# Pairs of 64-row matmuls, LN transposes by DMA and a DMA-shifted V in a fused attention and gated-MLP kernel

## The chip, the cores and the metric

The kernel runs on one core of one Trainium2 chip. The metric is device time in microseconds (us) of one launch; lower is better. Each version ran four or five times, interleaved with the kernel before (three to seven times) on the same chip, and medians are quoted with the lowest and highest time. "Span" is the length of the profiled execution from its first to its last instruction; the time of a launch is about 1.7 us longer.

## The reference

There are two blocks: a layer norm (LN), windowed attention and a residual; then a second LN, a gated MLP that mixes tokens with a 2048x2048 matrix, and a residual. All data is bf16.

```python
# x [2048, 448]; 16 heads of 28; window 8, dilation 2
qkv  = LN(x) @ wqkv                               # 448 -> 3*448
o    = softmax(q . k[pos - 2*(0..7)] * scale) @ v # eight keys per query, masked before 0
h    = x + o @ wo                                 # 448 -> 448
z    = gelu(LN(h) @ w_in)                         # 448 -> 1792
z1, z2 = z[:, :896], LN(z[:, 896:])
g    = w_sp @ z2 + b_sp[:, None]                  # 2048 x 2048 over the tokens
out  = h + (z1 * g) @ w_out                       # 896 -> 448
```

## The kernel before

The program is written as a graph of steps. Each step has one or more candidate engines with a modelled duration, the buffers it reads and writes, and a priority. A list scheduler in Python places the steps one after the other: it takes the engine that can start first, and on it the step of lowest priority number. The result is a fixed order of instructions for each engine, with semaphore waits between engines. All DMAs are issued by one queue (SyncE, SP), in order.

The parts that the change touches, with cuts:

```python
DC, NCH, NQ, PAD, NAB = 112, 4, 114, 14, 18    # K = 448 as four chunks of 112 rows
xhT = sb("xhT", [DC, NCH, TOKBUF], BF16)       # LN output, transposed, tokens contiguous

def layernorm(m, i, prio):                     # a block of 128 tokens
    ...                                        # statistics and normalise on VectorE -> tring
    # four transposes on PE, then one evacuation into xhT by ScalarE or VectorE

def qk_tile(tc, g8, prio):                     # z1 and z2 have the same form
    G.add([("pe", pe_us(4, 512))], [
        lambda e, c=c: e.matmul(bank(b, 512), wsrc[:, c, gg, :], xhT[0:DC, c, col0:col0 + 512],
                                start=(c == 0), stop=(c == NCH - 1)) for c in range(NCH)], ...)

def att_block(i):                              # 114 queries, 128 keys: 18 overlapping windows
    G.add([("pe", pe_us(4, D))], [             # V straight at the window's own tokens
        lambda e, c=c: e.matmul(bank(b, D, 0, nk), xhT[0:DC, c, t0:t0 + nk], stg[:, c, 2*D:3*D], ...)
        for c in range(NCH)], ...)
    ...                                        # logits, exp, mask, E @ V, transpose
```

Everything up to the last output projection (q/k, V, logits, exp, mask, E @ V, output projection, second LN) is called the attention stage here. After it come z2 with its LN, z1, and then the g and output matmuls.

The softmax here doesn't subtract the row's maximum and nothing guards it: scores larger than these inputs give would overflow.

## Time and profile before

| | before |
|---|---|
| time, median of 3 runs | 265.75 us (265.65 to 268.64) |
| PE / VectorE / ScalarE busy | 97 / 58 / 40% of the span |
| attention stage ends (last output projection) | 97.3 us |
| g and output matmuls end | 259.8 us |

From the page of the kernel before: the span, the busy times of the engines, the busy tenths of PE in 40 slices, the clock granted to PE in tenths, and what the chain of work that ended last consists of.

```profile
span 263.0 us, 4647 instructions
PE 255.1 (97%) x1868; PEld 129.8 (49%) x1868; DVE 152.4 (58%) x342; ACT 106.3 (40%) x204; POOL 46.6 (18%) x123
PE   6899999999998999999999999999999999999995
PEclk9999999999999999999999999999999999999999
PE 89%; DMA 3%; DVE 3%; ACT 2%; SPq 1%; POOL 1%; issue 0%; DVEq 0%
```

PE (the tensor engine) is the limit from beginning to end, at full clock. The windows view of the same kernel gives, for a stretch of time, its length and each engine's busy time in it, then the granted clock, the DMA share and GB/s:

```profile
60.00:80.00 20.00, 20.00 (x269) 12.24 (x267) 18.05 (x39) 17.20 (x36) 4.08 (x8) 1.00 0.01 2
97.20:117.50 20.30, 20.30 (x117) 10.87 (x117) 20.25 (x54) 14.17 (x26) 10.07 (x26) 1.00 0.25 46
```

In the middle of the attention stage PE is busy for all 20 us, VectorE (third pair of columns) for 18.05 and ScalarE for 17.20. A faster PE would soon meet them. Between 60 and 80 us the DMA queue does nothing (share 0.01). Three pieces of the chain of waits, in order of time (start, duration, what):

```profile
52.81 0.77 PE psum L535 x4
53.58 1.73 PE psum L524 x8
55.31 0.76 PE psum L596 x4
```

They are one V group, two q/k groups and one output projection. Each group pays for four matmuls, though K = 448 fills only 3.5.

### The profile page before, as it was taken

The numbers are of one execution on the slowest core, as the hardware profiler recorded it, in microseconds if no ns is written. First come the engines' busy times: TensorE is split into PE (matmuls) and PEld (weight loads), VectorE is DVE, ScalarE is ACT, GpSimd is POOL, SyncE is SP. The second block draws the span as 40 slices with busy tenths as digits, with TensorE's granted clock in tenths as the row PEclk, the third lists the DMA queues.
The fourth block names the chain that finished last, engine by engine and source line by source line (L and its number), as shares of the span: only waits on it lengthen the run. The fifth ranks groups of instructions, "written<-read, shape, count | busy, mean of one in ns | idle before, by whom it ended". The sixth has DMA issues, their size and how long they took to land.

```text
span 263.0 us, 4647 instructions
## 1 busy us (share of the span) xinstructions
PE 255.1 (97%) x1868; PEld 129.8 (49%) x1868; DVE 152.4 (58%) x342; ACT 106.3 (40%) x204; POOL 46.6 (18%) x123
## 2 busy tenths in 40 slices
PE   6899999999998999999999999999999999999995
PEld 2445665556655555554444444444544444444442
DVE  4697999979979999999431333131513133222233
ACT  1468979779979976772011000111010100010100
POOL 8676013221211125555000000000000000000000
PEclk9999999999999999999999999999999999999999
DMA  6999945000001213213000344401445200200002
GB/s 172 325 261 241 137 99 66 2 0 2 2 0 24 62 43 44 54 42 49 12 0 0 70 98 98 125 4 38 101 100 84 70 0 0 72 0 0 0 2 70
DMA packets 42182, 16.91 MB, mean 64 GB/s; under 512 B 35248, under 2 KB 41584, under 8 KB 42160
## 3 DMA queue, kind: packets, MB, share of 16 engines
q1 hardware_dynamic: 42160, 16.61, 29.3%
q8 instruction: 15, 0.25, 0.4%
q14 instruction: 7, 0.06, 0.1%
HBM read 6.37 MB, written 1.84 MB: 31 GB/s over the span
## 4 chain that ended last, share of the span: by engine, by line
PE 89%; DMA 3%; DVE 3%; ACT 2%; SPq 1%; POOL 1%; issue 0%; DVEq 0%
PE psum L667 37%; PE psum L524 10%; PE psum L632 9%; PE psum L654 9%; PE psum L685 8%; PE psum L596 4%; PE psum L535 4%; DMA x_tm<-in_A_x_dram 3%; PE psum L496 2%; PE psum L569 2%; PE psum L547 2%; ACT E L556 2%; PE psum L582 1%; DVE st L486 1%; DVE tring L491 1%; SPq L440 0%
## 5 line engine op out<-in xcount | busy, mean ns | idle before, releaser
L672 DVE TENSOR_TENSOR ub<-psum,bb 128x512 bf16<-128x512 f32 x28 | 19.4, 691 | 82.7 <-PE psum L667 82.7
L659 ACT ACTIVATE z1p<-psum 128x512 bf16<-128x512 f32 x28 | 16.7, 597 | 114.1 <-PE psum L654 114.1
L667 PE MATMUL psum<-wsp,z2p 128*128 128x512 bf16 x224 | 51.0, 379 | 0.0
L667 PE MATMUL psum<-early,z2p 128*128 128x512 bf16 x224 | 50.8, 379 | 0.0
L556 ACT ACTIVATE E<-psum 128x456 bf16<-128x456 f32 (+1 forms) x72 | 35.0, 562 | 1.4 <-PE psum L547 1.2
L667 PEld LDWEIGHTS psum<-wsp,z2p 128*128 128x128 bf16 x224 | 21.8, 98 | 26.5
L667 PEld LDWEIGHTS psum<-early,z2p 128*128 128x128 bf16 x224 | 21.9, 98 | 26.4
L524 PE MATMUL psum<-xhT,early 112*128 112x512 bf16 x128 | 30.5, 379 | 0.1
L654 PE MATMUL psum<-xhT,w_in 112*128 112x512 bf16 x112 | 28.8, 378 | 0.0
L514 POOL TENSOR_TENSOR rstd<-va,mhalf 128x1 f32<-128x1 f32 x48 | 27.7, 580 | 3.2
L512 POOL TENSOR_SCALAR va<-mv 128x1 f32<-128x1 f32 x48 | 13.2, 283 | 72.8 <-DVE mv L488 62.0
L632 PE MATMUL psum<-w_in,xhT 112*128 112x448 bf16 x128 | 25.5, 352 | 0.0
L685 PE MATMUL psum<-w_out,z1p 128*128 128x448 bf16 x112 | 21.8, 352 | 0.0
L486 DVE BATCH_NORM_STATS2 st<-x_tm 128x6 f32<-128x448 bf16 x32 | 19.2, 610 | 2.6 <-DMA x_tm<-in_A_x_dram 2.5
L637 ACT ACTIVATE z2p<-psum 128x448 bf16<-128x448 f32 x32 | 17.1, 544 | 7.2 <-PE psum L632 7.2
L564 DVE TENSOR_TENSOR E<-E,maskb 128x1824 bf16<-128x1824 bf16 (+1 forms) x18 | 19.6, 1089 | 0.0
L640 DVE BATCH_NORM_STATS2 st<-z2p 128x6 f32<-128x448 bf16 x32 | 18.1, 596 | 0.0
L654 PEld LDWEIGHTS psum<-xhT,w_in 112*128 112x128 bf16 x112 | 10.9, 97 | 13.3
L524 PEld LDWEIGHTS psum<-xhT,early 112*128 112x128 bf16 x128 | 11.5, 97 | 12.0 <-ACT V L508 0.2
L632 PEld LDWEIGHTS psum<-w_in,xhT 112*128 112x128 bf16 x128 | 12.1, 98 | 10.3
L535 PE MATMUL psum<-early,xhT 112*128 112x448 bf16 (+1 forms) x72 | 16.1, 352 | 0.8 <-DVE xhT L509 0.8
L685 PEld LDWEIGHTS psum<-w_out,z1p 128*128 128x128 bf16 x112 | 11.0, 98 | 10.4
(59 smaller groups left out, 245.7 us busy)
## 6 DMA issues: line engine op xcount, KB each, us to landing
out_dram<-tring SPq DMA_DIRECT2D x16, 112.0 KB, 1.8
w_in<-in_B_w_in_dram SPq DMA_DIRECT2D x1, 1568.0 KB, 13.8
x_tm<-in_A_x_dram SPq DMA_DIRECT2D x1, 896.0 KB, 10.0
early<-in_A_wqkv_dram SPq DMA_DIRECT2D x1, 784.0 KB, 6.0
w_out<-in_B_w_out_dram SPq DMA_DIRECT2D x1, 784.0 KB, 15.5
bb<-in_B_b_sp_dram SPq DMA_DIRECT2D x1, 512.0 KB, 13.2
wsp<-in_B_w_sp_dram SPq DMA_TRANSPOSE x32, 2.8
early<-in_B_w_sp_dram SPq DMA_TRANSPOSE x32, 2.7
```

The source lines that it names most:

```text
L486: G.add([("dve", dve_us(D))], [lambda e: e.bn_stats(st[:, s.slot, 0:6], x_tm[:, m, :])], [r_x[m]], [s], [s], prio=prio)
L514: G.add([("pool", 0.61)], [lambda e: e.tensor_tensor(rstd[:, k:k + 1], va[:, k:k + 1], mhalf[:, 0:1], ALU.pow)], [r_va[k], r_half], [r_rs[ ...
L524: lambda e, c=c: e.matmul(bank(b, 512), wsrc[:, c, gg, :], xhT[0:DC, c, col0:col0 + 512], start=(c == 0), stop=(c == NCH - 1)) for c in ra ...
L535: lambda e, c=c: e.matmul(bank(b, D, 0, nk), xhT[0:DC, c, t0:t0 + nk], stg[:, c, 2 * D:3 * D], start=(c == 0), stop=(c == NCH - 1)) for c ...
L556: lambda e, hh=hh: e.activation(E[0:nk, ev.slot, hh * 4:(hh + 1) * 4, 0:nq], bank(lb[hh], 512, 0, nk).rearrange("p (g c) -> p g c", c=128) ...
L564: lambda e: e.tensor_tensor(E[0:nk, ev.slot, :, 0:nq], E[0:nk, ev.slot, :, 0:nq], maskb[0:nk, mi:mi + 1, 0:nq].to_broadcast([nk, NHEAD, nq ...
L632: lambda e, c=c, b=b, h=h, m=m: e.matmul(bank(b, D), xhT[0:DC, c, PAD + 128 * m: PAD + 128 * m + 128], w_in[:, c, FH + D * h: FH + D * (h ...
L640: lambda e, h=h, m=m, s=s: e.bn_stats(st[:, s.slot, 6 * h:6 * h + 6], z2p[:, m, D * h:D * (h + 1)])],
L654: lambda e, c=c: e.matmul(bank(b, 512), w_in[:, c, fc * 128:(fc + 1) * 128], xhT[0:DC, c, PAD + 512 * tc: PAD + 512 * (tc + 1)], start=(c ...
L667: lambda e, s=s: e.matmul(bank(b, 512), z2p[:, s, fc * 128:(fc + 1) * 128], w[:, s, :], start=(s == 0), stop=(s == NB - 1)) for s in range ...
L672: G.add([("dve", dve_us(512))], [lambda e: e.tensor_tensor(ub[:, u.slot, :], bank(b, 512), bb[:, 512 * tc:512 * (tc + 1)], ALU.add)], [b, ...
L685: lambda e, f=f: e.matmul(bank(b, D), z1p[:, f, 128 * m:128 * m + 128], w_out[:, f, :], start=(f == 0), stop=(f == FC7 - 1)) for f in rang ...
```

## The change

The intent is to take work off PE. K = 448 becomes seven chunks of 64 rows. Two products are computed at once, one on the upper and one on the lower 64 rows of the array, in seven steps instead of two times four. The lower half needs the same data on the other 64 partitions, so there is a half-swapped copy xS of the transposed LN output xB. Most LN transposes move from PE to DMA. V is computed once per 128 tokens, in 16 groups rather than 18, and DMAs shift it into the 18 windows. The diff, cut to its core (weight layouts and loads, semaphore reuse and tile aliasing are left out):

```diff
-        xhT = sb("xhT", [DC, NCH, TOKBUF], BF16)
+        xB = sb("xB", [128, NB, NCH, 128], BF16)       # per block; chunks of 128,128,128,64 rows
+        xS = sb("xS", [128, NB, NCH, 128], BF16)       # the two 64-row halves swapped
         def layernorm(m, i, prio):
+            if i or m >= NPT:                          # NPT = 8: 24 of the 32 blocks
+                dma_t(lambda: xB[:, m, :, :], lambda: tring[:, t.slot, :], 1.26, ...)   # DMA transpose
+                if m % 2: ...                          # two DMAs swap the halves of a pair of blocks
+                return
             ...                                        # blocks 0 to 7: on PE as before,
+            ...                                        # and two half copies by VectorE or ScalarE
+        def pair(b, ws, xs, n):
+            return [lambda e, j=j, u=u: e.matmul(bank(b[j], n), ws(j, (LO, HI)[j], u), xs(j, (LO, HI)[j], u),
+                        start=(u == 0), stop=(u == 6), tile_position=(64 * j, 0)) for u in range(7) for j in range(2)]
+        def full(b, ws, xs, n):                        # V and the output projection
+            return [lambda e, c=c, ps=ps: e.matmul(bank(b, n), ws(ps, c), xs(ps, c), ...)
+                    for c, ps in ((0, ALL), (1, ALL), (2, ALL), (3, LO))]    # the last on 64 rows
+        def v_tile(m, prio): ...                       # V of 128 tokens -> ring Vt of 4 slots
         def att_block(i):
-            ...                                        # V at the window's own tokens
+                dma(lambda e, ...: e.dma_start(V1[p0:p0 + n, v.slot, :, :], Vt[q0:q0 + n, ...]),
+                    e1 - k0, [vbuf[m]], ...)           # 34 shifts, one or two per window
+        # model: a DMA costs max(0.45, kb/300) us of the queue and lands 1.7 us later;
+        # a change of tile mode on PE costs 0.1 us; warm-up matmuls are fillers of lowest priority
+        # all z1 pairs are placed before the g matmuls
```

## The prediction

> **What bounds the kernel now.** TensorE (PE). The page's busy line gives PE 255.1 of 263.0 us (97%), VectorE 58%, ScalarE 40%; the chain of waits is 89% PE. By windows, the attention stage (15 to 100 us) loads all three: PE 99%, VectorE about 78 of 85 us, ScalarE about 71. After it only PE is loaded.
>
> In the PE timeline a 512-column matmul costs 216 ns start to start, a 448-column one 189 ns, whether 112 or 128 rows are used. K=448 as 4x112 pays for 4 passes but fills 3.5.
>
> **What the change does to PE.**
> - q/k, z2, z1: a pair of tiles takes 7 steps of two 64-row matmuls in place of 8 full ones. If the halves overlap fully this saves 1/8: 27.6 to 24.2, 24.2 to 21.2, 24.2 to 21.2 us: -9.4 us. The Trainium skill ("TensorEngine Tiling (Array Packing)", Key Properties) says that tiles execute independently. This trace agrees for 32-row tiles: in the logits' matmuls groups of four tiles of 114 columns start about 50 ns apart, the time of one.
> - V: 18 overlapping blocks become 16, -1.5 us.
> - LN transposes: 24 of 32 blocks leave PE (0.22 to 0.27 us each): -6 us; their evacuations (0.60 us on ScalarE or 0.42 on VectorE) go too, about 12 us of the two engines.
> - Cost: the same section says that changing the tiling mode drains the array. Around the logits' matmuls about 0.1 us is lost each way; with an estimated 30 to 40 more switches: +3 to +4 us.
>
> Sum of PE work: about 244 before, 227 after, plus switches.
>
> **Elsewhere.** The start: x blocks 2 and 3 arrive late now (VectorE waits 2.1 us) and q/k begins at 14.8 us. Four blocks now come before the weights, and warm-up becomes filler: -1 to -2 us. Against it: 16 half copies (estimate 0.2 to 0.6 us each), and a DMA queue that gains 24 transposes (1.3 us each, from the batch of 16 in 21.1 us), about 35 V shifts and 24 swaps (0.4 to 0.5 us each): near 90 us of issue before attention ends, full but in time, as w_sp loads can slip behind z2/z1. Landing (1.8 to 2.8 us) lengthens each LN chain; other pairs cover it.
>
> **How much is critical.** Nearly all PE time. z2/z1: -6 us in full. The attention stage would lose about 11 us of PE work, but switches and VectorE/ScalarE (which lose only about 8 us net together) give back 3 to 5: about -7. Start: -1.5. Total about -15 us: 250.5 us, range 245 to 257. Faster by over 2%: 0.93; within 2%: 0.06; slower: 0.01.
>
> **What would show it.**
> - Groups by shape show 64-row matmuls, 224 each for q/k and z2, 196 for z1; a pair takes 1.5 us (512 columns) or 1.33 (448).
> - First q/k at 12 to 13.5 us; last output projection ends near 89 us (97.2 before); z1, now in one run, ends near 129; the g and output matmuls behind it keep about 118 us.
> - PE busy near 240 us; waits for VectorE, ScalarE or the V shift a few us; for w_sp none.
>
> **What would make it wrong.** The 64-row halves may not overlap fully (weight loads not hidden, or PSUM writes): at 1.7 us a pair the gain shrinks to about 7 us. The in-order DMA queue may block: a V shift or LN transpose behind w_sp transposes would stall PE. SBUF transposes may be slower than 1.3 us. Better than told: VectorE and ScalarE keep up, and the stage gets its whole 11 us.

## The result and the profile after

The time is **283.81 us** (median of 4 runs, 281.90 to 285.73) beside 265.7 us of the kernel before in the same rounds (264.77 to 268.64). The ratio is 1.0661, with a 95% interval from 1.0549 to 1.0773: slower. Ratios here are the mean time of one kernel's fast runs over that of the other's of the same rounds, so they are not quite the ratio of the medians that stand beside them. Executions over 1.5% slower than the fastest of the same kernel are left out of the means. The prediction was wrong in its direction.

The same lines of the page, after:

```profile
span 282.7 us, 5079 instructions
PE 258.9 (92%) x2036; PEld 119.9 (42%) x2036; DVE 155.9 (55%) x351; ACT 95.6 (34%) x187; POOL 51.6 (18%) x119
PE   6499977997699879997999999999999999999995
PEclk9689997999579978998899999999999999999999
PE 80%; DMA 6%; POOL 4%; DVE 3%; SPq 2%; ACT 2%; issue 1%; DVEq 0%; ACTq 0%; POOLq 0%
```

PE now has holes in the first half, and its clock drops there too. PE's busy time did not fall, because matmuls at half clock count double. The windows of the kernel after (columns as before) say where:

```profile
15.00:40.00 25.00, 24.92 (x256) 11.33 (x255) 22.03 (x62) 17.86 (x35) 10.18 (x24) 0.97 0.82 142
60.00:80.00 20.00, 15.79 (x156) 6.44 (x154) 11.40 (x25) 8.73 (x18) 3.04 (x6) 0.78 0.58 135
100.00:121.00 21.00, 19.55 (x229) 9.32 (x223) 17.82 (x39) 13.09 (x26) 6.05 (x10) 0.84 0.57 107
121.00:137.50 16.50, 13.90 (x127) 6.95 (x123) 16.39 (x45) 8.45 (x19) 9.32 (x24) 0.90 0.60 119
137.50:161.50 24.00, 23.96 (x225) 12.73 (x226) 9.58 (x24) 16.59 (x32) 5.34 (x13) 1.00 0.22 49
161.50:279.30 117.80, 117.80 (x561) 54.57 (x560) 39.35 (x70) 1.09 (x2) 0.00 (x0) 1.00 0.22 54
```

Between 60 and 80 us PE, VectorE and ScalarE are all busy for less time than before (15.79, 11.40 and 8.73 us against 20.00, 18.05 and 17.20). None of the three is full, so the stage waits for something else. The DMA share went from 0.01 to 0.58. From 137.5 us on nothing is wrong: 224 paired matmuls run without a gap in 24.0 us, and g with the output takes 117.8 us, where the prediction said about 118.

The last output projection ends at 121.1 us. It was 97.3 before, and the prediction said 89. So 32.1 of the 33.3 us between prediction and result had already arisen by the end of the attention stage.

The timelines show one of the stalls. First, the SP queue of the kernel after from 66 to 76 us. L413 is a DMA transpose, L611 a V shift (V1, Vt and other short-lived tiles share the memory of z1p and appear under its name), "x3" is three in a row.

```profile
66.44 1.29 SPq L413 DMA_TRANSPOSE xB<-tring  x1
67.78 2.40 SPq L611 DMA_DIRECT2D z1p<-z1p  x3
70.22 1.20 SPq L413 DMA_TRANSPOSE wsp<-in_B_w_sp_dram  x1
71.47 1.44 SPq L611 DMA_DIRECT2D z1p<-z1p  x2
72.95 1.21 SPq L413 DMA_TRANSPOSE xB<-tring  x1
74.20 1.26 SPq L413 DMA_TRANSPOSE wsp<-in_B_w_sp_dram  x1
```

Then ScalarE (ACT) in the same stretch of the kernel after; the brackets give the idle time before the instruction and what ended it:

```profile
70.61 0.54 ACT L552 ACTIVATE z1p<-psum 128x448 bf16<-128x448 f32 x1 [5.00 <-DMA z1p<-z1p]
74.95 0.54 ACT L552 ACTIVATE z1p<-psum 128x448 bf16<-128x448 f32 x1 [2.87 <-DMA z1p<-z1p]
```

And PE, again in the kernel after:

```profile
71.65 1.78 PE L575 MATMUL psum<-wo,qT 128*128 128x448 bf16 x4 [2.59 <-ACT qT L552]
75.55 1.79 PE L575 MATMUL psum<-early,xB 128*128 128x448 bf16 x4 [1.61 <-ACT z1p L552]
```

The chain of waits of the same stretch (start, duration, what) joins the three; "DMA" is a transfer from its issue to its landing:

```profile
69.38 0.79 SPq L611
70.22 1.20 SPq L413
71.47 3.38 DMA z1p<-z1p
74.95 0.55 ACT z1p L552
75.55 1.79 PE psum L575 x4
```

Read from the last line up: PE waits for ScalarE. ScalarE waits, for 5.00 and then 2.87 us, to copy V from PSUM into the ring Vt, because the slot is still being read by the shift of an older V. That shift was issued late: three shifts take 2.40 us of the queue where the model counted 0.45 each, and a transpose of w_sp that nobody needs before 160 us stands between them. Then it takes 3.38 us to land, where the model counted 0.45 of issue and 1.7. The queue also stands still itself: from 63.42 to 65.17 us it waits for an LN transpose to land, so that it may issue the swap, and the shifts stand behind. ScalarE is in order too, so the copy of the attention output into qT behind it, ready or not, waits as well. At 71.65 us four matmuls take 1.78 us, where such a group takes 1.03 us at 120.09 us in the same view: the clock has halved.

How much of the delay is queue and how much is landing? On the chain of waits from 15 us to the end of the stage the V shifts' way from issue to landing has 9.7 us in three pieces (2.33, 3.38 and 3.96), and the issue of transfers in front of them, other shifts included, 4.0 us. The chain is inferred, so this is a reading and not a test.

At the end of the stage the same queue is in the way a second time. The chain of waits of the kernel after, at the end of the second LN:

```profile
124.57 2.78 DMA early<-in_B_w_sp_dram
127.36 1.14 SPq L413
128.60 3.21 DMA xS<-xB
131.80 0.70 issue
132.50 4.51 PE psum L567 x28
```

PE waits for the swapped copy xS. Its swap stands in the queue behind transposes of w_sp, and the 28 matmuls then begin at half clock (by the clock records, from 132.7 to 136.1 us).

Summed over the queue's timeline up to 131 us, the 34 shifts take 26.3 us of issue (0.77 each), 23 LN transposes 30.3 (1.32 each), 22 swaps 14.5 (0.66 each), 18 w_sp transposes 24.0: with the loads 111.1 us. The prediction said near 90. In the other 20 us the queue stood idle or waited.

The Trainium skill ("TensorE: Matmul & The Clock Gate", Part 1, "What's actually happening") says that the clock is at half by default, and returns to it after an idle window of about 3.4 us. The trace agrees in the length: its clock records show half-clock stretches of 3.4, 6.8 and 10.2 us, multiples of such a window, 30.7 us in all. It does not show that PE must be idle for that long: the stretch that begins at 71.3 us falls into an idle time of 2.59 us, and in the 6 us before the one at 102.0 us PE was never idle for more than 1.02 us at a time. It remains to be found whether they are a cause or a symptom.

### The profile page after: what moved, and what is told of

Its sections match the earlier page's. It is cut to its first block, busy times and chain, and to the rows that moved or that the text cites. A ratio compares the mean times of both kernels' runs of the same rounds, so it can differ in the third digit from the quotient of the medians.

```text
span 282.7 us, 5079 instructions
## 1 busy us (share of the span) xinstructions
PE 258.9 (92%) x2036; PEld 119.9 (42%) x2036; DVE 155.9 (55%) x351; ACT 95.6 (34%) x187; POOL 51.6 (18%) x119
## 4 chain that ended last, share of the span: by engine, by line
PE 80%; DMA 6%; POOL 4%; DVE 3%; SPq 2%; ACT 2%; issue 1%; DVEq 0%; ACTq 0%; POOLq 0%
PE psum L742 34%; PE psum L567 23%; PE psum L575 10%; PE psum L760 7%; DMA z1p<-z1p 3%; PE psum L644 2%; PE psum L657 2%; DMA xS<-xB 1%; SPq L413 1%; DMA early<-in_B_w_sp_dram 1%; PE psum L622 1%; ACT qT L552 1%; SPq L534 1%; PE psum L539 1%; POOL rstd L558 1%
## 5 line engine op out<-in xcount | busy, mean ns | idle before, releaser
L631 ACT ACTIVATE z1p<-psum 128x456 bf16<-128x456 f32 (+1 forms) x72 | 35.7, 559 | 3.7 <-PE psum L622 3.3
L567 PE MATMUL psum<-xB,early 64*128 64x512 bf16 x112 | 29.5, 408 | 3.7 <-DVE z1p L553 3.7
L567 PE MATMUL psum<-xS,early 64*128 64x512 bf16 x112 | 29.6, 408 | 0.0
L567 PE MATMUL psum<-w,xB 64*128 64x448 bf16 x112 | 24.9, 382 | 2.6 <-DMA xS<-xB 2.1
L567 PE MATMUL psum<-w,xS 64*128 64x448 bf16 x112 | 25.0, 382 | 0.0
L575 PE MATMUL psum<-early,xB 128*128 128x448 bf16 x64 | 18.6, 396 | 4.2 <-ACT xB L552 2.3
L567 PE MATMUL psum<-xB,w 64*128 64x512 bf16 x98 | 21.3, 376 | 0.0
L567 PE MATMUL psum<-xS,w 64*128 64x512 bf16 x98 | 21.3, 376 | 0.0
L575 PE MATMUL psum<-wo,qT 128*128 128x448 bf16 x64 | 17.8, 379 | 2.7 <-ACT qT L552 2.6
L639 DVE TENSOR_TENSOR z1p<-z1p,maskb 128x1824 bf16<-128x1824 bf16 (+1 forms) x18 | 19.6, 1088 | 0.8 <-ACT z1p L631 0.8
```

Of the source, the lines that this page charges most:

```text
L567: return [lambda e, j=j, u=u: e.matmul(bank(b[j], n), ws(j, (LO, HI)[j], u), xs(j, (LO, HI)[j], u), start=(u == 0), stop=(u == 6), tile_po ...
L575: return [lambda e, c=c, ps=ps: e.matmul(bank(b, n), ws(ps, c), xs(ps, c), start=(c == 0), stop=(c == NCH - 1)) for c, ps in ((0, ALL), (1 ...
L631: lambda e, hh=hh: e.activation(E[0:nk, ev.slot, hh * 4:(hh + 1) * 4, 0:nq], bank(lb[hh], 512, 0, nk).rearrange("p (g c) -> p g c", c=128) ...
L639: lambda e: e.tensor_tensor(E[0:nk, ev.slot, :, 0:nq], E[0:nk, ev.slot, :, 0:nq], maskb[0:nk, mi:mi + 1, 0:nq].to_broadcast([nk, NHEAD, nq ...
```

## The experiments

At first three causes were in question: the V shifts in the DMA queue, the other transfers in it (transposes, swaps, w_sp), and tile mode changes on PE together with the halved clock. Every kernel gave correct results. Unless a kernel is named, diffs and differences are against the kernel after (283.81 us).

### First call: one part at a time

**tail128: the last matmul of V and output projection on 128 rows, 64 of them zeros.** In these groups three 128-row matmuls are followed by one of 64 rows, and that alone may count as a change of tile mode.

```diff
-  for c, ps in ((0, ALL), (1, ALL), (2, ALL), (3, LO))]
+  for c, ps in ((0, ALL), (1, ALL), (2, ALL), (3, ALL))]
+  ... two new GpSimd steps: memset wv[:, 3, :] and wo_sb[:, 3, :] to 0
```

> The changed kernel, but the last of the four matmuls of every V and output-projection group uses 128 rows (zero-filled) in place of 64. Theory M (switching the array between 128-row and 64-row tiles costs TensorE time): a group of four goes from 0.97 us back to 0.77 us, 32 groups, so about 6 us off: 277 us. Theory Q (TensorE waits for the one in-order DMA queue, and its clock is halved after such waits): TensorE time is not what ends last in the attention stage, so at most 3 us off: 281 to 284 us.

Measured: 290.55 us in the three fast runs (288.05 to 291.23), ratio 1.0916; the fourth, 292.5 us, is left out. It is 7 us slower, which no theory expected. The two memsets are new steps in the graph, and with them the scheduler changed the order of all engines. Whether the edit or the order did it is settled below (tail_same).

**wsp_late: the first 16 transposes of w_sp only behind the last swap of halves.**

```diff
-  load_wsp(0, wsp0, r_wsp[0], 30)
+  last_sw = [G.tasks[i] for i in r_xS[NB - 1].a_tasks]     # after the attention stage
+  load_wsp(0, wsp0, r_wsp[0], 30, after=last_sw)
```

> The changed kernel, but the first 16 w_sp transposes are issued only after the last half-swap DMA, so they no longer sit between the V shifts in the queue (20 us of issue leave the attention stage). Theory Q, if the w_sp loads are what delays the V shifts: 8 to 15 us off, 269 to 276 us. If the queue is blocked by the LN transposes and shifts themselves: under 4 us off. Theory M: no change, 284 us.

Measured: 281.62 us (280.85 to 282.8), ratio 1.0607: 2 us better. The gain lies behind the attention stage: the stage ends at 120.6 us (121.1 in the kernel after), and g begins at 158.3 (161.5). ScalarE and VectorE still wait 11.2 us for V shifts (13.9 in the kernel after, by the waits view). w_sp alone is not the cause.

**pe_transposes: all LN transposes back on PE, half copies on the engines.**

```diff
-  if i or m >= NPT:
+  if False:
```

> The changed kernel, but all 32 LN transposes go back to TensorE and all half copies to VectorE and ScalarE; V shifts stay on the queue. Theory Q: the queue loses 24 transposes of 1.3 us and 24 swaps of 0.6 us, 45 us in all, and the waits go: 265 to 272 us, although TensorE gets 6 us more work. Theory M: 6 us more TensorE work: about 290 us.

Measured: 289.35 us (287.78 to 289.73), ratio 1.0903. The expected gain did not come. LN transposes and swaps were gone from the queue, but w_sp and weights moved into the holes, and ScalarE still waited 7.4 us for V shifts (9.6 in the kernel after, by the waits view). In exchange PE and VectorE got the transposes and copies back: VectorE is busy for 173.5 us rather than 155.9. So taking the LN transposes off the queue does not pay here. What they cost inside the queue is not shown, since PE and VectorE got more work and the order changed.

**v_direct: no V shifts; xB contiguous in the tokens, V again at the 18 windows.** The pairs, the DMA transposes and the swaps stay.

```diff
-  xB = sb("xB", [128, NB, NCH, 128], BF16)
+  xB = sb("xB", [128, NCH, XO + S_TOK], BF16)                # XO = 16
-  v_tile(m, ...); dma(... V1[p0:p0 + n, ...], Vt[q0:q0 + n, ...])
+  e.matmul(bank(b, D, 0, nk), xB[ps, c, XO - PAD + t0:XO - PAD + t0 + nk], wv[ps, c, :], ...)
```

> The changed kernel, but the transposed LN outputs lie contiguous over tokens, so V is computed straight at the 18 overlapping windows as before the change; no V shift by DMA, no V ring behind it (26 us of issue leave the queue). Theory Q: 12 to 20 us off, 264 to 272 us, and the half-clock stretches in the attention stage mostly go. Theory M: 2 more groups of four, no gain: 284 to 286 us.

Measured: 268.50, 269.42 and 270.98 us in the three fast runs, ratio 1.0152 (1.0096 to 1.0207). That is 14.4 us better than the kernel after, by far the largest single step. The profiled run, the fourth, is left out: it took 873.71 us, and its chain of waits has lines such as

```profile
420.82 95.25 PE psum L733 x116
```

for 116 matmuls that take 25.14 us in the kernel after, 3.8 times as long. It shows nothing of the kernel, and so this run has no profile of the fast state; its successor v_direct128 has.

### Second call: what about the shifts, and what else?

**vshift_pool: the same shifts, issued by GpSimd.** If the place in the SP queue is the cause, taking them out of it should help.

```diff
-  dma(lambda e, ...: e.dma_start(V1[...], Vt[...]), ...)
+  G.add([("pool", 1.0)], [lambda e, ...: e.dma_start(V1[...], Vt[...])], ...)
```

> The changed kernel, but the 34 V shifts are issued by GpSimd, on a queue of their own, instead of the one in-order queue that also carries transposes, swaps and weight loads. Theory Q1 (a V shift is late because something ahead of it in the queue waits or takes its 1.3 us): the waits for V shifts mostly go, as in v_direct: 266 to 273 us. Theory Q2 (the shift's own issue-to-landing time of 2 to 3 us and the four-deep V ring are at fault, whatever queue): less than 5 us off, 279 to 284 us.

Measured: 289.90 us (288.66 to 292.48), ratio 1.0927: 6 us slower. The waits view shows why the test is confounded:

```profile
POOL z1p L614 <- DMA z1p<-z1p: 20.1, 9, 5.2
POOL z1p L614 <- PE psum L647: 16.7, 10, 8.6
```

(engine, line, what it waited for: us in total, times, longest). GpSimd is in order as well, and it computes the LNs' rstd. While it waits, up to 8.6 us, to be allowed to issue a shift, the LNs wait behind it. From GpSimd a shift landed 2.7 us after its issue in the median (1.9 to 8.2), by the tile view. The run shows that one in-order queue was exchanged for another; it does not settle what part position has.

**fill_stalls: 43 dummy matmuls at the largest stalls, so that the clock stays up.** The order of everything else is unchanged.

```diff
+  FILL = {12: 5, 16: 8, 50: 14, 81: 10, 83: 6}    # before the n-th PE step, so many dummies
```

> The changed kernel with 43 dummy 512-column matmuls put into the TensorE stream right where its five long waits before 80 us were seen (5, 8, 14, 10, 6 of them), so that TensorE is not idle there. Theory C (the halved clock after each long wait is a large part of the loss): the half-clock stretches at 10, 44 and 71 us go and about 8 us come off: 275 to 277 us. Theory N (the stage is paced by the queue, so a faster TensorE only waits longer): under 2 us off, 282 to 285 us.

Measured: 286.31 us (284.02 to 286.72), ratio 1.0755. The strip of the granted clock of this kernel, and its window from 40 to 60 us:

```profile
PEclk9999999999799968999799999999999999999999
40.00:60.00 20.00, 18.40 (x215) 8.29 (x213) 14.44 (x29) 11.23 (x23) 3.99 (x6) 1.00 0.54 115
```

The clock was at 1.00 there (0.91 in the kernel after), and over the whole run the mean rose from 0.946 to 0.976. The time went up by 2.5 us. Until the attention stage ended PE ran at half clock for 10.2 us rather than 27.3, and yet the stage ended at 121.4 us rather than 121.1. So in this stage the halved clock is a symptom of waiting and not what sets the time: what PE does faster, it then waits for longer (V evacuations on ScalarE waited 13.7 us for shifts rather than 9.6). The matmul that stood at 46.5 us in the kernel after came 2.3 us earlier, and the one at 71.65 us 0.9 us later. The dummies did not hold up the V group of 75.55 us: here too it begins 0.60 us after the start of ScalarE's copy (75.86 to 76.46; 74.95 to 75.55 in the kernel after).

**v_direct128: v_direct plus the 128-row last matmul.**

```diff
   # on v_direct
-  for c, ps in ((0, ALL), (1, ALL), (2, ALL), (3, LO))]
+  for c, ps in ((0, ALL), (1, ALL), (2, ALL), (3, ALL))]      # + the two memsets
```

> v_direct with the last matmul of every V and output-projection group on 128 zero-filled rows instead of 64. With the V shifts gone TensorE should be the limit again in more of the stage, so theory M, which tail128 alone could not test under the queue's waits, should now show: 34 groups by 0.2 us, 4 to 7 us off v_direct's 269.4: 262 to 266 us. If mode switches inside a group are hidden: no change.

Measured: 264.36 us (263.13 to 266.94), ratio 0.9965: 5 us better than v_direct. Now the kernel is level with the one before. The two memsets changed the order of all engines here too, so the 5 us are edit and order together; a clean test follows (best2_tail64). In its profile the last output projection ends at 98.0 us.

**v_pe128: v_direct128 with all LN transposes on PE.**

```diff
   # on v_direct128
-  if i or m >= NPT:
+  if False:
```

> v_direct128 with all 32 LN transposes on TensorE and the half copies on VectorE and ScalarE, so that the queue carries only loads and stores. If the LN transposes and swaps on the queue still stall TensorE after the V shifts are gone: faster than v_direct128 by 2 us or more. If not: slower by 4 to 10 us, from 6 us of TensorE work and about 18 us of half copies and 12 us of evacuations shared by VectorE and ScalarE: 266 to 275 us.

Measured: 269.63 us (268.45 to 271.14), ratio 1.0154: 5.3 us slower than v_direct128. VectorE is busy for 168.5 us rather than 153.2. So the DMA transposes and swaps do pay by themselves; without the V shifts the queue has room for them.

### Third call: the size of a shift, the end of the stage, the start

**vshift_16: windows of 112 queries and 16 rows of padding, so that all shifts are of a multiple of 16 rows.** The shifts of the kernel after have such sizes as 126, 116 or 86 rows. The Trainium skill ("DMA: Bandwidth & Descriptors", "Why a DMA increments its semaphore by 16 and not by 1") says that a DMA is divided over the largest number of engines, at most 16, that divides the size of its slowest dimension: 116 rows would get 4 engines and 86 only 2. The idea was that such shifts land late.

```diff
-  NQ, PAD, NAB = 114, 14, 18
+  NQ, PAD, NAB = 112, 16, 19
```

> The changed kernel with attention blocks of 112 queries and a 16-token pad in place of 114 and 14, so that every V shift moves a multiple of 16 rows (one more block, 19 in place of 18, about 1 us of TensorE and 2 us each of ScalarE and VectorE). Theory S (shifts whose row count has no large factor are spread over few of the 16 DMA engines and land late, up to 4 us): the V waits shrink and 5 to 10 us come off, 274 to 279 us. Theory Q1 (position in the queue): no gain, 283 to 288 us with the extra block.

Measured: 285.76 us (282.82 to 286.74), ratio 1.0725. The shifts did get cheaper: a median issue of 0.59 us rather than 0.77, landing after 2.1 us in the median (1.8 to 4.7). The kept trace bears the rule out, though no view shows it: in the kernel after, the landing of a shift raises its semaphore in 16 steps for 112 rows, 15 for 126, 5 for 116 and 3 for 86, which is always one more than the rule's number of engines where that is under 16. By these records the 11 shifts for which the rule gives 6 engines or fewer landed after 3.7 us in the median, the other 23 after 2.3. The time did not follow all the same. But there is one window more, and the order changed, so a small gain from the sizes may be hidden.

**vd_tail: on v_direct128, statistics of z2 on VectorE wait for the last second LN.** In v_direct128 the in-order VectorE ran z2 statistics ahead of the last LNs, and PE then waited for xS.

```diff
   # on v_direct128
-  e.bn_stats(st[...], z2p[...]) ... prio=p)
+  e.bn_stats(st[...], z2p[...]) ... prio=p, after=[ln_done[-1]])
```

> v_direct128, but the statistics of z2 on VectorE wait until the last LN of h is normalised. Theory T (at the end of attention VectorE is filled with z2 statistics, the last LN of h is late, TensorE waits 5 us for the last half swap and then runs at half clock): 5 to 8 us off v_direct128's 264.4: 257 to 260 us. If the last swap is late by the queue alone: under 2 us off.

Measured: 262.63 us (262.21 to 264.41), ratio 0.9886: 1.7 us better, less than the 5 to 8 hoped for. The waits view names the one that was left, first in v_direct128:

```profile
PE psum L570 <- DMA xS<-xB: 5.2, 2, 3.2
```

and in vd_tail:

```profile
PE psum L573 <- DMA xS<-xB: 5.0, 2, 3.7
```

The wait for the swap did not go: now the w_sp transposes stood in front of it.

**vd_start: on v_direct128, the memsets of attention tiles later and ScalarE's table load earlier.** The chain of waits of the kernel after begins with GpSimd: five memsets, 1.74 and 4 times 0.34 us, stand in front of the first rstd.

```diff
   # on v_direct128
-  memset V1, E, otm at the start
+  the same memsets, after=[rstd of block 3];  an early Exp on one column (ACT)
+  ... wo_sb[:, 3, :] is set behind the weight loads, at a more urgent priority
```

> v_direct128, but GpSimd sets the pads of V, E and O after the first four LN reciprocal roots instead of before, and ScalarE loads its table on a dummy at the start instead of at 9.6 us. Theory B (the start is late by these, first q/k pair at 15 to 19 us): 2 to 4 us off, 260 to 262 us. If VectorE and ScalarE limit the stage behind it, the gain is lost again: 263 to 265 us.

Measured: 270.47 us (268.97 to 271.32), ratio 1.0162. The first q/k pair did come earlier (15.79 us rather than 17.02), but the run is 6 us slower, since the order behind it had changed everywhere. What a better start is worth remains open.

**best1: vd_tail, vd_start and wsp_late together.**

```diff
   # on vd_tail: + vd_start's late memsets and early table load, + wsp_late's after=last_sw
```

> v_direct128 with both of these and the first w_sp loads behind the last half swap. If the parts add: 254 to 258 us, faster than the kernel before the change by 3 to 4 percent; if VectorE limits the attention stage: 258 to 262 us.

Measured: 264.08 us (262.76 to 264.12), ratio 0.9912. Its difference from best2 below is the edit of the start alone, and that costs it 6 us again.

### Fourth call: order against cost

**tail_same: the edit of tail128 with the order kept.** The zeros are written inside two existing GpSimd steps, so the graph is the same; the order was compared for every engine and is the same.

```diff
-  for c, ps in ((0, ALL), (1, ALL), (2, ALL), (3, LO))]
+  for c, ps in ((0, ALL), (1, ALL), (2, ALL), (3, ALL))]
+  ... both memsets appended to steps that are there already
```

> Same edit as tail128 (128 zero-filled rows in the last matmul of each V and output-projection group), but with the two fills put into existing GpSimd steps, so that the order of instructions on every engine stays that of the changed kernel; tail128 had reshuffled the whole order. Theory M: the groups fall from 0.97 to 0.77 us and with nothing else changed 2 to 6 us come off: 278 to 282 us. If tail128's loss came from the 128-row form itself and not from its order: 288 to 291 us again.

Measured: 283.33 us (282.77 to 285.34), ratio 1.0639: 0.5 us better than the kernel after, within its spread. So tail128's loss of 7 us was its order. And in the kernel after itself the 64-row matmul costs nearly nothing, as PE waits there anyway.

**model_true: only the scheduler's numbers changed.** The same work, and the measured costs in the model.

```diff
-  max(0.45, kb / 300.0)                    # queue time of a DMA
+  max(0.6, kb / 300.0)                     # a V shift: 0.8
-  pe_us(4, D)                              # V and output projection groups
+  pe_us(4, D) + 0.2
```

> The changed kernel with only three constants of its schedule changed to what the trace shows: 0.8 us of queue per V shift and at least 0.6 per other transfer (it assumed 0.45), and 0.2 us more per V and output-projection group. The work is the same, only the order differs. Theory O (the order was planned on a queue that is too cheap, so w_sp and weight transfers were slipped in before shifts): 6 to 12 us off, 272 to 278 us. If the order is not at fault but the shifts as such: within 4 us of 283.8.

Measured: 277.47 us (276.23 to 277.72), ratio 1.0397. The order alone is worth 6.3 us. That it is better because the costs are true is argued: tail128, whose order changed for another reason, moved as far the other way. The last output projection now ends at 111.8 us rather than 121.1.

**best2: vd_tail with the first 16 w_sp transposes behind the last swap** (best1 without the edit of the start). Against vd_tail only the order of the queue differs.

```diff
   # on vd_tail
-  load_wsp(0, wsp0, r_wsp[0], 30)
+  load_wsp(0, wsp0, r_wsp[0], 30, after=last_sw)
```

> vd_tail with the first w_sp loads behind the last half swap. vd_tail still waited 5 us for the last half swaps, so if w_sp transposes ahead in the queue are what delays them: 257 to 260 us, over 2 percent faster than before. If not: 261 to 264 us.

Measured: **258.13 us** (257.99 to 259.26), ratio **0.9695** (0.9609 to 0.9781). It beats both kernels. From its page:

```profile
span 256.2 us, 5058 instructions
PE 244.7 (95%) x2044; PEld 117.6 (46%) x2044; DVE 153.7 (60%) x349; ACT 97.6 (38%) x192; POOL 47.0 (18%) x120
PE   6699989999999799999999999999999999999995
PEclk9899999999999999999999999999999999999999
```

and from its windows:

```profile
15.00:97.00 82.00, 78.40 (x1077) 40.53 (x1074) 77.18 (x183) 64.84 (x131) 24.24 (x52) 1.00 0.58 110
97.00:135.00 38.00, 38.00 (x370) 17.94 (x368) 27.74 (x71) 26.83 (x52) 14.52 (x36) 1.00 0.48 98
135.00:252.80 117.80, 117.80 (x562) 54.63 (x560) 39.36 (x70) 1.08 (x2) 0.00 (x0) 1.00 0.24 58
```

PE is whole again, and no wait of PE for xS is left. Yet the attention stage ends at 97.9 us, where it had ended at 97.3 before: **all of the gain lies behind it.** From there to the run of g it takes 37.2 us (97.9 to 135.1), and 44.5 before (97.3 to 141.8, taken as 259.8 less the 118.0 that g and output take in best2). Of these 7.3 us about 1.7 are z2 work that best2 does before the mark (58 of its 224 z2 matmuls; 24 of 128 before), by estimate from the counts. In the attention stage VectorE is busy for 77.2 of 82 us and PE for 78.4.

**best3: best2 with 0.6 us as the least queue time of a DMA in the model.**

```diff
-  max(0.45, kb / 300.0)
+  max(0.6, kb / 300.0)
```

> best2 with at least 0.6 us of queue assumed per transfer in place of 0.45. If a truer plan helps: 256 to 259 us; if the plan does not matter once the V shifts are gone: as best2 within 2 us.

Measured: 259.81 us (258.96 to 262.95), ratio 0.9733: no better. Without shifts the queue's model no longer matters much.

### Fifth call: clean costs at best2

**best2_tail64: the 64-row last matmul put back into best2.** The order is the same on every engine.

```diff
   # on best2
-  for c, ps in ((0, ALL), (1, ALL), (2, ALL), (3, ALL))]
+  for c, ps in ((0, ALL), (1, ALL), (2, ALL), (3, LO))]
```

> best2 with the 64-row last matmul back in every V and output-projection group, nothing else; the order of instructions on every engine is that of best2. Theory M where TensorE does not wait for shifts: 34 groups by 0.2 us, 3 to 7 us slower than best2's 258.1: 261 to 265 us. If VectorE paces the attention stage and hides it: under 2 us slower.

Measured: 262.38 us (262.10 to 263.41), ratio 0.9871: 4.25 us slower. Its chain of waits has for a V and an output projection group

```profile
54.38 0.87 PE psum L581 x4
55.26 0.97 PE psum L585 x4
```

and best2 at the same place

```profile
52.70 0.77 PE psum L581 x4
53.46 0.76 PE psum L585 x4
```

There are 34 such groups, so 4.25 us are 0.125 us for each. **A matmul with half its rows in a group of full ones costs time; padding it with zeros to 128 rows costs nothing here.** The two runs stand in different calls; the kernel before had medians of 265.66 and 265.75 us beside them.

**best2_warm14: 14 warm-up matmuls rather than 24.** They hold a PSUM bank until far into the attention stage.

```diff
-  NWARM = 24
+  NWARM = 14
```

> best2 with 14 warm-up matmuls in place of 24. The last of the 24 run late in the attention stage and hold one of the 8 PSUM banks until then. If that bank limits the stage: 2 to 4 us off, 254 to 256 us. If not: 257 to 260 us, or slower if the missing fillers let the clock drop.

Measured: 259.33 us (258.90 to 259.86), ratio 0.9756. No sign that the bank limits; the order changed here too.

## Why the prediction was wrong

**The sum of it.** The prediction missed by 33.3 us (283.8 against 250.5). One chain of kernels divides it:

| step | from | to | us |
|---|---|---|---|
| no V shifts by DMA (v_direct) | 283.8 | 269.4 | -14.4 |
| 64-row last matmul padded to 128 (v_direct128) | 269.4 | 264.4 | -5.0 |
| end of the stage: z2 statistics and w_sp behind the last LN and swap (vd_tail, best2) | 264.4 | 258.1 | -6.2 |
| not recovered | 258.1 | 250.5 | -7.6 |

The steps are not independent of each other: padding the last matmul gave 0.5 us in the kernel after (tail_same), 5.0 on v_direct and 4.25 at best2, and the first two edits of this table also changed the order of every engine. (In the third PE and ScalarE kept theirs.) The order alone was seen to make 7.2 us (tail128 against tail_same).

**"... near 90 us of issue before attention ends, full but in time, as w_sp loads can slip behind z2/z1."** This is the step that failed. The issue was 111.1 us, since a shift took 0.77 us rather than 0.4 to 0.5 and a swap 0.66. And the sum was the wrong question: a queue that is free for a while can still be in the way at the moment that counts. The w_sp loads did not slip behind; the scheduler put them wherever its model saw a hole. "What would make it wrong" named this ("a V shift or LN transpose behind w_sp transposes would stall PE"), but gave it no weight: the chance of slower was 0.01. Nor was w_sp the main part of it: its first 16 transposes cost about 2 us (wsp_late), the V shifts 14.4 (v_direct).

**"Landing (1.8 to 2.8 us) lengthens each LN chain; other pairs cover it"** and **"waits for ... the V shift a few us".** The landing times were right for swaps and transposes (medians of 2.4 and 2.7 us) but not for the shifts on few engines (3.7). What failed is that others cover it. A shift is three waits in a row: one on the queue to be issued, one to land, one for the ring slot to be free for the next V. The engines that wait, ScalarE and VectorE, are in order, and took the attention's copies with them. The clock's half rate then followed, as a consequence (fill_stalls).

What part of the shifts' 14.4 us is which? The order of the model took 6.3 us back without any change of work (model_true). The 8 us that remain, either queue position or latency, were not separated: vshift_pool, which should have done that, only exchanged one blocked queue for another. The chain of waits of the kernel after speaks for latency (9.7 us from issue to landing, 4.0 for the issue of what stood in front), but no run tests it. vshift_16 shortened the landing without a gain in time, beside one window more and another order.

**"If the halves overlap fully this saves 1/8".** Right. In the PE timeline of the kernel after, a pair of 64-row matmuls of 512 columns starts every 0.22 us (the first q/k pair at 19.14, 19.36, 19.58 us), as a single one of 112 rows did before (0.216). The Trainium skill ("TensorEngine Tiling (Array Packing)", Key Properties) has tiles that execute independently, and the trace agrees for 64 rows. z2 and z1 were to bring 6 us; at best2 the stretch from the end of attention to the run of g is 7.3 us shorter, or about 5.6 without the z2 work done earlier.

**"with an estimated 30 to 40 more switches: +3 to +4 us".** The size was of the right order, the count was not. The prediction missed that each V and output projection group ends with a 64-row matmul. That was worth 4.25 us, 0.125 per group (best2_tail64); that it is a change of mode is the natural reading, but no run shows the drain itself. Also, inside the attention stage a q/k pair takes 1.62 us at best2, between other modes, against 1.73 for the two groups before, where 1/8 less would be 1.51: there, half of the gain is lost, presumably to switching.

**"The attention stage would lose about 11 us of PE work, but switches and VectorE/ScalarE ... give back 3 to 5: about -7."** Even at best2 the stage ends at 97.9 us, not near 89. The first q/k pair comes at 16.95 us (18.7 in the kernel after) rather than at 12 to 13.5, and at 14.76 before: the start was mis-sized by about 4 us. The V groups are 18 again, which undoes the 1.5 us. And VectorE did not lose work: 77.2 of 82 us, against 75.2 of the 82.2 us from 15 to 97.2 before. That VectorE is now the limit of this stage is argued from these numbers; PE is busy for 78.4 of the 82 us too, and the run that adds VectorE work (v_pe128, +5.3 us) fits, but adds PE work as well. The prediction's own marks (z1 ends near 129, 118 us behind it, some 3 us of stores, 1.7 from span to time) give a time nearer 252 than 250.5, so a further 1 us or so of the remainder is its arithmetic.

**"the g and output matmuls behind it keep about 118 us"** was right (117.8).

## What to carry to other kernels

Before moving work from a full engine to an in-order DMA queue, ask of each transfer which two steps of the critical chain stand on either side of it, and what can stand in front of it in the queue at that moment; the sum of the queue's time says little. Compare edits at equal order: here the same edit gave -0.5 us or +7 us. Measured issue times in the scheduler's model gave 6.3 us once (model_true) and nothing where the shifts were gone (best3). In a group of full-height matmuls pad the last chunk with zeros rather than use fewer rows.

## What the Trainium skill lacked or had wrong

- "TensorEngine Tiling (Array Packing)", Key Properties, says that changing mode drains the array but not how much it costs, nor whether an ordinary matmul on 64 rows at the end of a group of 128-row ones counts as a change. The runs show 0.87 to 0.97 us rather than 0.77 for such a group of four, 4.25 us for 34 of them.
- "DMA: Bandwidth & Descriptors" gives no trn2 issue time of a small copy within SBUF or of a transpose from SBUF to SBUF (it has cycles of "previous generations" in a part on trn3). Here a shift of up to 126 rows took 0.77 us of the queue, 0.59 in the median where all sizes were multiples of 16, and a transpose of 128x512 bf16 1.26 to 1.32 us, landing after 2.7 in the median.
- The same page's rule for how many engines a DMA uses led to the idea of vshift_16. The trace agrees with the rule (3 steps of the semaphore for 86 rows, 5 for 116, 16 for 112). The page does not say what few engines cost a small copy: here 3.7 us to land with 6 engines or fewer, 2.3 with more. The kernel got no faster from better sizes (285.76 against 283.81 us).
- "TensorE: Matmul & The Clock Gate", "Seeing it yourself", warns of a clock stuck at a quarter for 50 us and more. One execution here (v_direct) ran 3.8 times too slow in its matmuls and took 873.71 us, with no clock change in its records (mean 1.0): the page has no case that lasts a whole execution.
- The same page has the clock return to half after an idle window of about 3.4 us. The trace shows it halved for 30.7 us in all, once with no idle time above 1.02 us in the 6 us before. No page says that removing them need not help: with the clock at 0.976 rather than 0.946 the time was 286.31 rather than 283.81 us.
